# Transforming u for both halves of a column block in one step of the feed

## The chip, the cores and the metric

The kernel runs on one core of a Trainium2 chip. TensorE (PE in the profile) multiplies matrices, its weight loads are counted apart (PEld); VectorE (DVE), ScalarE (ACT) and GpSimd (POOL) work on tiles; SyncE (SP) issues nearly all transfers. The metric is the device time of one execution in microseconds, of which the median of several runs is taken.

## What is computed

Two mixers read the same input `u` (2048 rows of 448) and a gate per row mixes them. The first is a state-space convolution: a kernel `K` of 2048 taps per channel is built from 256 decaying complex modes and convolved with `u` by FFT. The second is attention in four segments of 512 rows with a memory that is carried from segment to segment.

```python
# A: state-space convolution
P = exp((A * dt)[:, :, None] * pos)            # 448 x 256 x 2048
K = 2 * einsum("dn,dnl->dl", C, P).real
a = irfft(rfft(u, 2L) * rfft(K, 2L))[:L] + u * D_skip
# B: four segments, 16 heads of 28
q, k, v = x @ wq, x @ wk, x @ wv
for s in range(4):
    a_dot = softmax(q_s k_s^T * scale + causal) v_s
    a_mem = (phi(q_s) M) / (phi(q_s) z)
    o_s = g * a_mem + (1 - g) * a_dot
    M, z = M + phi(k_s)^T v_s, z + sum(phi(k_s))
b = o @ wo
out = sigmoid(u . gate_w) * a + (1 - that) * b
```

## The kernel before

**Two halves.** The first half (to about 444 us of the profile) builds the taps of `K`, makes all projections q, k, v, the memory of each segment, and the first step of the transform of `u`. The second half loads what the first left in HBM, transforms `K` (`transform_k`, matmuls `ps_a<-kb,s1k`), finishes the FFT and runs the attention. Its first rows are the loads of the mask `mk` (L1573) and of `qu` and `ku` (L1393), all issued by SP.

**The taps.** `first_half` (L309) runs 56 steps n. A step has `turns` (eight small bf16 matmuls into `ps_arg`), `trig` on ACT (two rounds and one sine, tile `cs`), `product` on DVE (X at L393, Y at L397, L398, L399) and `sums` on PE (64 matmuls `ps_k<-Y,X`). Behind every fourth step stands a group: ACT loads its exponential table, makes six `decay` tiles (EY, EX) from `ps_arg`, the taps are copied to `kb` (L420), and ACT loads the table for sines again. ACT and DVE run in the order in which the code calls them (`k.strict`); PE always does.

**The feed.** All other work of the first half comes out of a generator, `project` (L680), a step at a time. `Feed.spend` (L483) releases steps until their modelled cost has used up the allowance `RATES` of the stage; a step yields its cost, and "pe" means a hold: two units of a projection are in PSUM, and no more is released until `exps` makes room. For each segment s the generator loads four tiles `xin` (L852), turns them on PE into `xh` and `xl` (L1382), makes `values`, then units of q and k (nine matmuls `ps_m<-xh,w` and `ps_m<-xl,w`). A unit's result is emptied by `e` and `hi` on ACT and by `ph` and `lo` on DVE (L765, L767); `memory` adds four matmuls `ps_m<-v,pkT`, emptied on DVE into `tm` and `macc` (L810, L811).

**The transform of u.** `transform_u` (L513) is a second generator, the `filling`. A step of it takes one half h of one column block w: one fp32 matmul on the 64 rows of that half, `ps_m<-ut,s1u`, into a buffer of the PSUM tag "m", a copy to `gs` (on ACT, or on DVE while `k.exps` is set) and a DMA to GU in HBM (L538). There are 32 steps. They are taken at the start of each segment but the first, in twos on either side of `memory` in the units called light (L907 on), by `spend` where a hold leaves allowance over, by `fill` at the end of the steps (L450, L456), and what is left by `rest`. The blocks `ut` are loaded two ahead, in three buffers. `gs` takes three buffers of its own, and from w = 12 on the half h = 1 takes one of the four `xin` buffers.

**PSUM.** The tag "m" has three buffers in the first half (L1507). Transposes, values, units, memory and the transform of u all take them in turn; a matmul waits until the buffer that it is given has been emptied.

Of the kernel before, what the change touches and what calls it, by code (L numbers as in the profile page):

```python
# [308 lines left out]
def first_half(nc, k, gy, feed):  # L309
# [21 lines left out]
    def load(J):  # L331
        if J < NJ:
            load_decay(J)
            load_phase(J)
# [26 lines left out]
    def turns(n):  # L361

        J, c = divmod(n, 2)
        arg[n] = pt = k.ps("arg")
        for nt in range(2):
            r, kw = rows(nt)
            k.mm(pt[:, nt], lt[J][r, c], k.ct[r, 0], start=True, stop=False, **kw)
        for i in range(2):
            for nt in range(2):
                r, kw = rows(nt)  # L370
                k.mm(pt[:, nt], k.one[r], k.mag[r, i : i + 1].broadcast_to([64, 512]), start=False, stop=False, **kw)
        for nt in range(2):
            r, kw = rows(nt)
            k.mm(pt[:, nt], lt[J][r, c], k.ct[r, 1], start=False, stop=True, **kw)

    def trig(n):

        pt = arg.pop(n)
        cs[n] = t = gw.tile([128, 2, 2, 2, 256], F32, tag="cs", name="cs", bufs=2)
        pv = pt.rearrange("p t (w c) -> p t w c", w=2)  # L380
        act(t[:, 1].rearrange("p w t c -> p t w c"), pv, AF.Sin, scale=TWO_PI)
        act(t[:, 0].rearrange("p w t c -> p t w c"), pv, AF.Abs)
        fl = t[:, 0].rearrange("p w t c -> p (w t c)")
        act(fl, fl, AF.Sin, bias=k.bhp, scale=-TWO_PI)

    def product(n):
        J, c = divmod(n, 2)
        t = cs.pop(n)
        X = gw.tile([128, 2, 2, 256], F32, tag="X", name="X", bufs=2)
        Y = gw.tile([128, 2, 16, 64], F32, tag="Y", name="Y", bufs=2)  # L390
        XY[n] = X, Y
        ex = EX[J][:, :, 256 * c : 256 * c + 256].unsqueeze(1).broadcast_to([128, 2, 2, 256])
        v.tensor_tensor(X, ex, t[:, :, 0], ALU.mult)  # L393
        ey = EY.pop((J, c)).rearrange("p t (d c) -> p (t d) c", c=64)
        y = t[:, :, 1].rearrange("p r t (d c) -> p r (t d) c", c=32)
        lo = ey[:, :, :32].unsqueeze(1).broadcast_to([128, 2, 16, 32])
        v.tensor_tensor(Y[:, :, :, :32], lo, y[:, :, :, ::-1], ALU.mult)  # L397
        v.tensor_tensor(Y[:, 0, :, 32:], ey[:, :, 32:], y[:, 0], ALU.mult)  # L398
        v.scalar_tensor_tensor(Y[:, 1, :, 32:], ey[:, :, 32:], -1.0, y[:, 1], ALU.mult, ALU.mult)  # L399
# [39 lines left out]
    for n in range(2 * NJ):  # L439
        if n < 4:  # L440
            load(n + 2)
        elif n % 2 == 0:
            load(n // 2 + 4)
        if n % 4 < 3:
            turns(n + 1)
        trig(n)
        feed.spend(1.7 * RATES[n // 4])
        product(n)
        if n == 2 * NJ - 1:
            feed.fill(2)  # L450
        if n % 4 > 0:
            sums(n - 1)
        if n % 4 == 3 and n + 1 < 2 * NJ:
            decays(n // 4 + 1)
            turns(n + 1)
    feed.fill(4)  # L456
    sums(2 * NJ - 1)


# [53 lines left out]
def transform_u(nc, k, up, pp):  # L513

    uv = k.u.rearrange("(n h w) d -> h n w d", h=2, w=16)
    guv = k.GU.rearrange("k r (h w) d -> h (k r) w d", h=2)
    def load(w):
        ut = up.tile([128, D], F32, tag="ut", name="ut", bufs=3)
        for h in range(2):
            nc.sync.dma_start(ut[64 * h : 64 * h + 64], uv[h, :, w])  # L520
        return ut

    uts = {0: load(0), 1: load(1)}
    for w in range(16):
        if w < 14:
            uts[w + 2] = load(w + 2)
        ut = uts.pop(w)
        for h in range(2):
            pt = k.ps("m")
            k.mm(  # L530
                pt[:, :D], k.s1u[64 * h : 64 * h + 64], ut[64 * h : 64 * h + 64],
                start=True, stop=True,
            )

            where, tag, bufs = (pp, "xin", 4) if w >= 12 and h else (up, "gs", 3)
            gs = where.tile([128, D], F32, tag=tag, name="gs", bufs=bufs)
            k.copy(gs, pt[:, :D], AF.Copy)
            nc.sync.dma_start(guv[h, :, w], gs)  # L538
            yield 0.9


def transform_k(nc, k, fp):
# [137 lines left out]
def project(nc, k, pp, early, filling):  # L680
# [72 lines left out]
    def high(u, pt):  # L753
        hi = pp.tile([128, SEG], F32R, tag="hi", name="hi", bufs=2)
        if u[2] == 0:
            copy(hi, pt, AF.Copy)
        else:
            copy(hi, pt, AF.Identity, bias=k.po)
        return hi
# [78 lines left out]
    def remember():  # L838
        while pending:
            u, ph = pending.pop(0)  # L840
            yield from memory(u, ph)
            yield 1.0 - 0.4 * u[2]

    for s in range(NSEG):
        if s > 0:
            yield -next(filling, 0.1)
        xh = pp.tile([112, 4, SEG], F32R, tag="xh", name="xh")
        xl = pp.tile([112, 4, SEG], F32R, tag="xl", name="xl")
        for t in range(4):
            xin = pp.tile([128, D], F32, tag="xin", name="xin", bufs=4)  # L850
            with k.issue_after(holds[s]) if s in holds else ExitStack():
                nc.sync.dma_start(xin, k.u[SEG * s + 128 * t : SEG * s + 128 * t + 128])  # L852
            pt = k.ps("m")
            for kt in range(4):
                k.tr(
                    pt[:112, 128 * kt : 128 * kt + 128], xin[:, 112 * kt : 112 * kt + 112], k.ident
                )
            pv = pt[:112].rearrange("p (k q) -> p k q", k=4)
            ts_ = slice(128 * t, 128 * t + 128)
            copy(xh[:, :, ts_], pv, AF.Copy)  # L860
            v.tensor_tensor(xl[:, :, ts_], pv, xh[:, :, ts_], ALU.subtract)
            yield -1.0 if s == 0 or t % 2 else 1.0
        yield from remember()
        if s > 0:
            yield from values(s, xh, xl, range(1))
        if s == 0:
            split = weights()
            for _ in range(4):
                yield next(split)

        if s == 0:
            plain = [(s, h, 0) for h in range(4)]
            units = [(s, h, 1) for h in range(4)]
        elif s == 3:
            plain = [(s, h, 1) for h in range(4)]
            units = [(s, h, 0) for h in range(4)]
        else:
            plain = []
            units = [(s, h, m) for h in range(4) for m in range(2)]
        order = plain + units if s == 0 else units + plain  # L880
        after = dict(zip(order, order[1:] + [None]))
        x = (xh, xl)

        def rest_of(us):
            for u in us:
                pt = yield from matmuls(u, x)
                load_w(after[u])
                store(u, pt, high(u, pt))
                yield -0.7

        if s == 0:
            yield from values(s, xh, xl, range(4))
            for x_ in split:
                yield -0.3
                k.turn_over(k.ps("m"), 3)
                yield 0.6
            yield from rest_of(plain)
        for i in range(0, len(units), 2):
            us = units[i : i + 2]
            pts = []  # L900
            light = i == 2 if s == 0 else i > 2 and s < 3
            if s > 0 and i == 2:
                yield from values(s, xh, xl, range(1, 4))
                store_v(s)
            for u in us:
                if pts:
                    for _ in range(2 if light else 0):  # L907
                        yield -next(filling, 0.1)
                    yield from remember()
                    for _ in range(2 if light else 0):  # L910
                        yield -next(filling, 0.1)
                pts.append((yield from matmuls(u, x)))
                load_w(after[u])
                yield 0.65
            yield "pe"
            es, his, phs = [], [], []
            for u, pt in zip(us, pts):
                es.append(raised(pt))
                his.append(high(u, pt))
            for u, pt, e, hi in zip(us, pts, es, his):  # L920
                phs.append(phi(pt, e))
                store(u, pt, hi)
            if s == 0 and i == 0:
                store_v(s)
            pending += zip(us, phs)
            yield 0.1
        if s == 3:
            yield from rest_of(plain)
# [692 lines left out]
```

## Time and profile before

| | |
|---|---|
| median of 3 runs | 852.42 us (850.0 to 855.2) |
| span of the profiled execution | 850.4 us |
| PE busy | 750.1 us, 88% of the span |
| DVE busy | 582.0 us, 68% |
| ACT busy | 538.6 us, 63% |
| POOL busy | 171.8 us, 20% |
| DMA moved | 152.98 MB, 180 GB/s in the mean |

The shares are means over two halves with different limits. A stage is read from the table of windows (busy time of each engine between two times, with PEclk, the clock that the throttle granted to TensorE, 1.00 being full speed), and in it from the timeline: start, duration, engine, line, tiles and, in brackets, the idle time before a row and what ended it. The chain of waits follows the work that ended last back from the end of the kernel. Several instructions in a row of one kind are one line of the timeline (x64).

### The profile page before, as it was taken

What the parts mean: (1) busy time and instruction counts of PE and PEld (TensorE: products, weight loads), DVE (VectorE), ACT (ScalarE), POOL (GpSimd) and SP (SyncE); (2) the same over time, 40 slices, a digit from 0 to 9 for tenths busy, and PEclk for the clock granted to TensorE, in tenths of its full rate; (3) what the DMA queues carried; (4) which work ended last, traced back from release to release, by engine and by line L of the source; (5) the groups of instructions that cost most, each with busy time, mean ns of one, the idle gap of its engine ahead of it and who ended that gap; (6) DMA issues with size and microseconds to landing.
All of it is one profiled execution on the core that took longest, in us unless ns stands there. A gap on an engine that the chain in (4) does not pass through costs nothing.

```text
span 850.4 us, 19021 instructions
## 1 busy us (share of the span) xinstructions
PE 750.1 (88%) x7608; PEld 405.1 (48%) x7608; DVE 582.0 (68%) x1143; ACT 538.6 (63%) x638; POOL 171.8 (20%) x217
## 2 busy tenths in 40 slices
PE   1686987998879989899988999989997998988997
PEld 1363655764546655566643444434443444343443
DVE  8878678767788676876687765656565757563474
ACT  4867889799998989898863255554453444521320
POOL 5314111011110111001110121341115113331110
PEclk9589999999999989799999899999999999979899
DMA  9347853325642346314558967667466645654872
GB/s 248 91 108 237 247 186 112 99 91 172 197 143 85 104 153 200 132 46 149 178 202 349 349 221 235 204 220 233 118 219 220 194 152 182 210 205 152 223 231 97
DMA packets 88290, 152.98 MB, mean 180 GB/s; under 512 B 20626, under 2 KB 57162, under 8 KB 88154
## 3 DMA queue, kind: packets, MB, share of 16 engines
q1 hardware_dynamic: 79130, 140.83, 51.7%
q10 hardware_dynamic: 7424, 9.18, 3.1%
q0 software_dynamic: 1648, 1.76, 0.8%
q8 instruction: 60, 0.98, 0.5%
q14 instruction: 28, 0.23, 0.1%
HBM read 90.87 MB, written 60.63 MB: 178 GB/s over the span
## 4 chain that ended last, share of the span: by engine, by line
PE 54%; ACT 16%; DVE 15%; DMA 7%; issue 6%; POOL 1%; SPq 1%; ACTq 0%; DVEq 0%; POOLq 0%
PE ps_a L1379 19%; PE ps_m L1379 17%; PE ps_pv L1379 8%; ACT cs L1344 7%; PE ps_arg L1379 5%; PE ps_k L1379 3%; DVE jk L994 3%; DVE Y L397 2%; ACT L1344 2%; PE ps_m L1382 2%; DVE Y L398 1%; DVE X L393 1%; DMA xt<-in_A_u 1%; ACT EX L1344 1%; DMA ident<-in_c_id 1%
## 5 line engine op out<-in xcount | busy, mean ns | idle before, releaser
L994 DVE CUSTOM_DVE_ANT_0 jk<-ps_a,mk 128x512 f32<-128x512 f32 (+3 forms) x256 | 124.9, 488 | 71.0 <-PE ps_a L1379 63.7
L1024 ACT ACTIVATE PT<-ps_a 128x1024 f32<-128x1024 f32 (+1 forms) x96 | 84.5, 881 | 118.6 <-PE ps_a L1379 112.0
L359 POOL TENSOR_TENSOR EX<-EX,cab 128x1024 f32<-128x1024 f32 x28 | 53.5, 1913 | 309.1 <-ACT EX L1344 244.8
L1344 ACT ACTIVATE cs<-ps_arg 128x1024 f32<-128x1024 f32 x111 | 107.3, 1021 | 0.6 <-DVE Y L398 0.3
L1379 PE MATMUL ps_m<-xh,w 112*128 112x512 f32 x256 | 92.9, 412 | 0.4 <-DVE lo L765 0.4
L1379 PE MATMUL ps_a<-qu,ku 32*128 32x512 f32 (+3 forms) x768 | 89.3, 353 | 1.7 <-DVE mx L994 1.4
L1035 POOL TENSOR_SCALAR_AFFINE_SELECT PT<-PT 128x256 f32<-128x256 f32 (+1 forms) x96 | 46.5, 485 | 206.5 <-ACT PT L1024 206.4
L393 DVE TENSOR_TENSOR X<-EX,cs 128x1024 f32<-128x1024 f32 x56 | 68.3, 1220 | 25.4 <-ACT cs L1344 25.4
L1379 PE MATMUL ps_k<-Y,X 128*32 128x64 f32 x3584 | 64.1, 226 | 9.0 <-DVE Y L398 8.8
L1379 PEld LDWEIGHTS ps_k<-Y,X 128*32 128x32 f32 x3584 | 54.9, 113 | 35.2 <-DVE Y L398 16.1
L397 DVE TENSOR_TENSOR Y<-EY,cs 128x1024 f32<-128x1024 f32 x56 | 70.0, 1250 | 0.0
L1379 PEld LDWEIGHTS ps_a<-qu,ku 32*128 32x128 f32 x768 | 62.4, 194 | 12.4 <-DVE mx L994 4.7
L1344 ACT ACTIVATE cs<-cs,bhp 128x1024 f32<-128x1024 f32 x56 | 64.5, 1151 | 1.8
L399 DVE SCALAR_TENSOR_TENSOR Y<-EY,cs 128x512 f32<-128x512 f32 x56 | 41.0, 732 | 31.2 <-ACT cs L1344 29.1
L1344 ACT ACTIVATE EY<-ps_arg 128x1024 f32<-128x1024 f32 x52 | 53.1, 1031 | 11.1 <-PE ps_arg L1379 10.1
L1379 PEld LDWEIGHTS ps_m<-xh,w 112*128 112x128 f32 x256 | 48.0, 188 | 19.7 <-issue 7.6
L1379 PE MATMUL ps_a<-ku,qu 32*128 32x512 f32 (+3 forms) x256 | 46.0, 394 | 12.3 <-DVE mx L994 9.9
L1379 PE MATMUL ps_arg<-ct,lh 64*128 64x512 bf16 x224 | 43.6, 387 | 9.0 <-ACT cs L1344 5.7
L1379 PE MATMUL ps_m<-xl,w 112*128 112x512 f32 x128 | 50.3, 393 | 0.0
L1379 PEld LDWEIGHTS ps_a<-ku,qu 32*128 32x128 f32 x256 | 22.2, 189 | 58.7 <-DVE mx L994 27.0
L1379 PEld LDWEIGHTS <-lh 64*128 64x128 bf16 x392 | 22.2, 95 | 53.4 <-issue 39.8
L606 DVE TENSOR_TENSOR pr<-ps_a,ks 128x896 f32<-128x896 f32 x32 | 34.8, 1087 | 17.7 <-PE ps_a L1379 17.0
(212 smaller groups left out, 1395.3 us busy)
## 6 DMA issues: line engine op xcount, KB each, us to landing
w<-WD SPq DMA_DIRECT2D x32, 448.0 KB, 4.7
qu<-QD SPq DMA_DIRECT2D x16, 512.0 KB
ku<-KD SPq DMA_DIRECT2D x16, 512.0 KB
GU<-gs SPq DMA_DIRECT2D x32, 224.0 KB, 2.5
GK<-gs SPq DMA_DIRECT2D x8, 896.0 KB, 5.1
gk<-GK SPq DMA_DIRECT2D x32, 224.0 KB, 4.7
gu<-GU SPq DMA_DIRECT2D x32, 224.0 KB, 3.7
BB<-bs ACTq DMA_DIRECT2D x16, 448.0 KB, 2.6
```

The costliest lines, as they stand in the source:

```text
L359: nc.gpsimd.tensor_tensor(o, o, cab, ALU.mult)
L393: v.tensor_tensor(X, ex, t[:, :, 0], ALU.mult)
L397: v.tensor_tensor(Y[:, :, :, :32], lo, y[:, :, :, ::-1], ALU.mult)
L398: v.tensor_tensor(Y[:, 0, :, 32:], ey[:, :, 32:], y[:, 0], ALU.mult)
L399: v.scalar_tensor_tensor(Y[:, 1, :, 32:], ey[:, :, 32:], -1.0, y[:, 1], ALU.mult, ALU.mult)
L606: nc.vector.tensor_tensor(pr[c], pt, ks.pop(c), ALU.mult)
L994: v.tensor_tensor_reduce(junk[:, :n], pt[:, x, o : o + n], k.mk[:, SEG - n :], 1.0, -3e38, ALU.add, ALU.max, mx[:, 3 - t, h : h + 1],)
L1024: nc.scalar.activation(PT[:, 2 * hp : 2 * hp + 2, 512 * b : 512 * b + n], pt[:, :, :n], AF.Exp, scale=SCALE)
L1035: nc.gpsimd.affine_select(sl, sl, pat, ALU.is_ge, 0.0, base=0, channel_multiplier=-1)
L1344: x = op(*args, **kw)
L1379: tc.keep_in_program_order(nc.tensor.matmul(*args, **kw))
L1382: tc.keep_in_program_order(nc.tensor.transpose(*args))
```

## The change

A step of the transform of u now makes both halves of a column block: two PSUM buffers are taken, the two matmuls are issued one behind the other on the upper and the lower 64 rows of TensorE, then the two copies and the two DMAs. There are 16 steps, and a step's modelled cost is 1.5 where two steps of before had 1.8. Where the code took two steps it takes one, where four two; at the start of a segment and in `spend` it takes one step as before, which is now two halves.

```diff
         if n == 2 * NJ - 1:
-            feed.fill(2)
+            feed.fill(1)
...
-    feed.fill(4)
+    feed.fill(2)
     sums(2 * NJ - 1)
...
-        for h in range(2):
-            pt = k.ps("m")
+        pts = [k.ps("m") for _ in range(2)]
+        for h, pt in enumerate(pts):
             k.mm(
                 pt[:, :D], k.s1u[64 * h : 64 * h + 64], ut[64 * h : 64 * h + 64],
                 start=True, stop=True,
             )
-
+        for h, pt in enumerate(pts):
             where, tag, bufs = (pp, "xin", 4) if w >= 12 and h else (up, "gs", 3)
             gs = where.tile([128, D], F32, tag=tag, name="gs", bufs=bufs)
             k.copy(gs, pt[:, :D], AF.Copy)
             nc.sync.dma_start(guv[h, :, w], gs)
-            yield 0.9
+        yield 1.5
...
                 if pts:
-                    for _ in range(2 if light else 0):
+                    for _ in range(1 if light else 0):
                         yield -next(filling, 0.1)
                     yield from remember()
-                    for _ in range(2 if light else 0):
+                    for _ in range(1 if light else 0):
                         yield -next(filling, 0.1)
```

The instructions stand elsewhere in the queues than before, at three places above all. The first is the memory update of segment 1, ACT's queue: `cs` are the tiles of `trig`, `gs` the copies of the transformed u, `pkT` belongs to `memory`. Before:

```order
L1344 ACTIVATE pkT<-ps_m 128x512
L1344 ACTIVATE cs<-ps_arg 128x2x2x256 x2
L1344 ACTIVATE cs<-cs,bhp 128x1024
L1344 ACTIVATE gs<-ps_m 128x448
L1344 ACTIVATE cs<-ps_arg 128x2x2x256 x2
L1344 ACTIVATE cs<-cs,bhp 128x1024
L1344 ACTIVATE gs<-ps_m 128x448
L1344 ACTIVATE cs<-ps_arg 128x2x2x256 x2
```

With the change:

```order
L1344 ACTIVATE pkT<-ps_m 128x512
L1344 ACTIVATE cs<-ps_arg 128x2x2x256 x2
L1344 ACTIVATE cs<-cs,bhp 128x1024
L1344 ACTIVATE gs<-ps_m 128x448 x2
L1344 ACTIVATE cs<-ps_arg 128x2x2x256 x2
L1344 ACTIVATE cs<-cs,bhp 128x1024
```

The two copies, which stood behind two steps of `trig`, now stand behind one, and the next `trig` is queued behind both.

The second is the start of segment 3, SP's queue: `xin` are the four tiles that the segment's transposes read, QD and KD the stores of q and k. Before:

```order
L770 DMA QD<-hi 128x512
L852 DMA xin<-in_A_u 128x448 x2
L770 DMA KD<-hi 128x512
L852 DMA xin<-in_A_u 128x448 x2
L770 DMA QD<-lo 128x512
```

With the change:

```order
L770 DMA QD<-hi 128x512
L770 DMA KD<-hi 128x512
L770 DMA QD<-lo 128x512
L538 DMA GU<-gs 128x448
L770 DMA KD<-lo 128x512
L852 DMA xin<-in_A_u 128x448
L538 DMA GU<-gs 128x448
L852 DMA xin<-in_A_u 128x448 x2
L322 DMA lh_92<-SD 48x128 x2
L852 DMA xin<-in_A_u 128x448
```

The four loads, which stood among the stores of an earlier pair of units, now stand behind the stores of the last pair of u.

The third is the end of the first half, PE's queue, with the sums of the last three steps and the first matmuls of the second half. Before:

```order
L1379 MATMUL ps_m<-ph,macc_205 128x512
L1379 MATMUL ps_m<-ph,macc_206 128x512
L1379 MATMUL ps_m<-ut,s1u 128x448
L1379 MATMUL ps_k<-Y,X 32x64 x32
L1379 MATMUL ps_m<-ut,s1u 128x448 x3
L1379 MATMUL ps_k<-Y,X 32x64 x32
L1379 MATMUL ps_m<-ut,s1u 128x448 x4
L1379 MATMUL ps_k<-Y,X 32x64 x32
L1379 MATMUL ps_m<-ut,s1u 128x448
L1379 MATMUL ps_a<-kb,s1k 128x448 x16
```

With the change:

```order
L1379 MATMUL ps_m<-xl,w 128x512
L1379 MATMUL ps_m<-xh,w 128x512
L1379 MATMUL ps_k<-Y,X 32x64 x32
L1379 MATMUL ps_m<-ph,macc_205 128x512
L1379 MATMUL ps_m<-ph,macc_206 128x512
L1379 MATMUL ps_k<-Y,X 32x64 x64
L1379 MATMUL ps_a<-kb,s1k 128x448 x16
```

The nine halves of u that stood between the last sums are gone from there (all 16 pairs come before the transposes of segment 3), and the nine matmuls of one unit, the last two of which are shown, have come in ahead of them.

## The prediction

> **What bounds the kernel now.** I read the page first, then the windows of the first half, where the whole change lies, then the timeline at the places where u is transformed, and last the chain of waits at the end of that half.
>
> ```profile
> span 850.4 us, 19021 instructions
> PE 750.1 (88%) x7608; PEld 405.1 (48%) x7608; DVE 582.0 (68%) x1143; ACT 538.6 (63%) x638; POOL 171.8 (20%) x217
> 100.00:240.00 140.00, 125.37 (x1888) 80.72 (x1888) 108.70 (x152) 127.75 (x146) 19.12 (x10) 1.00 0.45 145
> 240.00:252.00 12.00, 9.76 (x165) 5.60 (x166) 11.08 (x18) 10.82 (x15) 1.99 (x2) 0.86 0.52 170
> 252.00:352.00 100.00, 92.87 (x1274) 59.05 (x1270) 72.25 (x101) 88.77 (x100) 13.32 (x7) 0.93 0.40 129
> 352.00:364.00 12.00, 9.83 (x165) 5.49 (x166) 10.94 (x17) 10.67 (x15) 2.03 (x2) 0.86 0.44 150
> ```
>
> The columns of the windows are length, busy time of PE, PEld, DVE, ACT and POOL, granted clock, DMA share and GB/s. The page's 88% of PE would make TensorE the bound and any saving on it a gain. The windows say otherwise for the first half: from 100 to 240 us ACT is busy 127.75 of 140.00 (91%), PE 125.37 (90%), DVE 78%; from 252 to 352 PE has 93%, ACT 89%. PE and ACT are level, and work passes from one to the other. In the two 12 us windows, the exponential phases at the start of segments 2 and 3, DVE and ACT are at about 90% and PE at 82%, and the clock fell to 0.86.
>
> **What the pairing can save.** These are all matmuls of u, the copies, and places where one, two and three halves run behind one another (a half is fp32 and has two passes, hence x2 and x64):
>
> ```profile
> L1379 PE MATMUL ps_m<-ut,s1u 64*128 64x448 f32 x64 | 31.4, 598 | 3.1 <-DVE lo L767 1.5 <-DMA ut<-in_A_u 0.7 <-DVE lo L765 0.5
> L1344 ACT ACTIVATE gs<-ps_m 128x448 f32<-128x448 f32 x19 | 10.2, 542 | 7.2 <-PE ps_m L1379 7.2
> L1344 DVE COPY gs<-ps_m 128x448 f32<-128x448 f32 x13 | 8.0, 619 | 2.7 <-PE ps_m L1379 2.2 <-DMA KD<-hi 0.5
> 432.23 1.02 PE L1379 MATMUL ps_m<-ut,s1u 64*128 64x448 f32 x2 [0.73 <-DVE lo L767]
> 434.20 1.77 PE L1379 MATMUL ps_m<-ut,s1u 64*128 64x448 f32 x6
> 543.57 1.02 PE L1379 MATMUL ps_a<-gk,cf 64*128 64x448 f32 x4 [0.36 <-DVE pr L606]
> ```
>
> One half alone takes 1.02 us from start to end. Three take 1.77: one of them added 0.75, another nothing. At 543.57 four passes of the same shape on both row halves take the same 1.02 as two. So a pair whose buffers are both free costs what one half costs, and saves 0.75 us of PE: 16 x 0.75 = 12.0 us at most. The copies are the same 32, of 0.54 us on ACT or 0.62 on DVE.
>
> But both buffers must be free at once, and the tag "m" has three. By the order of the allocations, which the code fixes, at none of the 16 pairs does the second half find a buffer that was surely empty before. For seven it is one that DVE empties with `lo` of a unit just made; for five it is the one that `tm` or `macc` of the memory update empties; for four it is the one of their own first half, so that the second half waits for the first one's copy. PE works in order and stands still meanwhile, with sums or decays queued behind.
>
> The Trainium skill, "TensorEngine Tiling (Array Packing)", section "Restrictions and Gotchas", names this as the price of row tiling: row tiles write to different PSUM banks, so the pressure on PSUM grows. That weighs against the change; the numbers that follow are from rows alone.
>
> **Seven pairs behind `lo`.** The wait of 0.73 us at 432.23 is such a wait of a single half, so a pair may lose 0.73 or gain 0.75: for seven -5.3 to +5.1. The holds make PE wait for `lo` in any case, so I take near nothing: +0.8.
>
> **Five pairs in the memory updates.** Segment 1, before:
>
> ```profile
> 204.62 1.16 PE L1379 MATMUL ps_m<-v,pkT 128*128 128x128 f32 x8 [1.11 <-ACT pkT L1344]
> 205.71 1.02 PE L1379 MATMUL ps_m<-ut,s1u 64*128 64x448 f32 x2
> 207.18 0.28 DVE L810 TENSOR_TENSOR tm<-ps_m,bm 128x128 f32<-128x128 f32 x1
> 207.48 0.53 ACT L1344 ACTIVATE gs<-ps_m 128x448 f32<-128x448 f32 x1
> 207.90 1.93 ACT L1344 ACTIVATE cs<-ps_arg 128x1024 f32<-128x1024 f32 x2
> 210.92 0.52 ACT L1344 ACTIVATE gs<-ps_m 128x448 f32<-128x448 f32 x1
> 211.18 1.22 DVE L393 TENSOR_TENSOR X<-EX,cs 128x1024 f32<-128x1024 f32 x1
> 211.34 1.93 ACT L1344 ACTIVATE cs<-ps_arg 128x1024 f32<-128x1024 f32 x2
> ```
>
> One half stood behind `v,pkT`, and its copy filled a slot of ACT. Now the second half follows at once, but its buffer comes free when `tm` ends: 207.18 + 0.28 = 207.46. Its 0.9 to 1.0 us end it at 208.4, its copy lasts to 208.9, and `trig`, queued behind both copies, starts at 208.9 instead of 207.90: +1.0. The later copy at 210.92 is gone (-0.45). X at 211.18, which waits for `trig`, and everything behind it moves by 0.5 to 1.0. Meanwhile `sums` and `turns` wait behind the second half on PE. Five times 0.7: +3.5 (0 to 5.2).
>
> **The starts of the segments.** A start takes one step, now a pair instead of a half, and further ones by `spend`. Where the second half waits for its own first one's copy, a matmul and a copy come on top: 1.02 + 0.53 = 1.55. For segment 1 I take this: +1.55 (0 to 1.55). Segment 2 gets four copies where it had one, 3 x 0.54 = 1.6 us on an ACT that has 1.2 us left in its 12 us window: +1.0 (0.4 to 2.6). Segment 3 has more:
>
> ```profile
> 327.61 0.90 SPq L852 DMA_DIRECT2D xin<-in_A_u  x2
> 351.80 1.28 ACT L1344 ACT_TABLE_LOAD   x1
> 356.01 0.58 ACT L1344 ACTIVATE gs<-ps_m 128x448 f32<-128x448 f32 x1
> 356.65 1.09 PE L1382 MATMUL ps_m<-ident,xin 128*112 128x128 f32 x8 [2.17 <-ACT gs L1344]
> 359.89 1.02 ACT L1344 ACTIVATE EY<-ps_arg 128x1024 f32<-128x1024 f32 x1 [0.46 <-PE ps_arg L1379]
> 361.38 1.03 ACT L1344 ACTIVATE EY<-ps_arg 128x1024 f32<-128x1024 f32 x1 [0.47 <-PE ps_arg L1379]
> 363.82 1.28 ACT L1344 ACT_TABLE_LOAD   x1
> ut<-in_A_u SPq DMA_DIRECT2D x32, 112.0 KB, 3.6
> ```
>
> Before, `xin` was loaded 29 us ahead (327.61) and turned at 356.65, 4.85 us after the table load. Now the loads stand in SP's queue behind the stores of the last pairs, and their buffers are those of the halves h = 1. In the same clock: the first copy of the pair at 356.0, the second half 1.02 later and its copy to 358.1, a decay of 1.05, two copies of the last pair to 360.2, a store of `lo` and the issue to 360.9, and 3.6 us to landing (of the loads of u, `ut`): 364.5, 12.6 after the table load instead of 4.85. Three of the six decays stand behind these transposes on PE; with 0.55 for the first transposes, the step of 359.89 to 361.38 twice and one decay, the phase ends 16.8 after the table load instead of 363.82 - 351.80 = 12.0: +4.8 (0 if the loads are not late, 7.6 if all that they are late remains).
>
> **Sum of the loops.** The steps between have fewer halves, and one unit leaves for the end of the half: nine matmuls, some 2 us of PE where PE has up to 93%, -1.5. So 0.8 + 3.5 + 1.55 + 1.0 + 4.8 - 1.5 = 10.15. ACT at 90% hides little of it, but PE and DVE catch up some: I let three quarters through, +7.6. In the 12 us windows a gap of 2.17 us went with a clock of 0.86, so a longer gap may cost (1 - 0.86) x 12 = 1.7 us again: +1.5 (0 to 2).
>
> **The end of the first half** gains:
>
> ```profile
> 436.71 3.85 DMA ut<-in_A_u
> 441.69 1.03 PE ps_k L1379 x64
> 442.72 0.96 PE ps_m L1379 x2
> 443.71 0.55 ACT gs L1344
> 444.69 0.38 SPq L1573
> 445.62 5.47 DMA ku<-KD
> 451.18 0.85 PE ps_a L1379 x5
> 439.15 0.68 DVE L398 TENSOR_TENSOR Y<-EY,cs 128x512 f32<-128x512 f32 x1
> ```
>
> This is the chain of waits but for its last row, which is of the timeline. The last halves wait for `ut` (3.85 us), the last sums for them, the load of `mk` (L1573) for the last half's copy and store, and the attention's first rows at 451.18 for `ku` behind it. With no half left, the last sums wait for the last product only, 439.15 + 0.68 = 439.83, end at about 440.9, and `mk` goes out at 441.1 instead of 444.69: -3.6 (0 if the unit that has come in delays the products as much).
>
> Total: +7.6 + 1.5 - 3.6 = +5.5 on 850.4, 855.9. The profiled execution is 2.0 under the median of the runs, so 852.42 + 5.5 = **858 us**.
>
> **Rivals.**
> 1. *The pairs run together as meant.* For it: 434.20 shows that the array does it, and 12 of the 16 pairs hold a second buffer of another kind. Against it: what empties that buffer comes late. Saved would be 12.0 us of PE, of which half lies on the path while PE and ACT are level, 6, and 3.6 at the end, less some 2 at segment 3: 850.4 - 7.6 and 2.0 more is 845. The Trainium skill, "TensorE: Matmul & The Clock Gate", "Part 3: Packing small matmuls", says that matmuls start and end strictly in order. Held to for every pass, a pair would take three passes and save half of the 0.75; the row of 543.57 does not agree with that.
> 2. *Absorbed.* The waits of PE fall where it would wait for ACT in any case, and the loops lose 3.6, what the end gains: 852.
> 3. *Segment 3 decides* (slower, more than forecast). One mechanism: the loads of `xin` land at 12.6 us after the table load, and the whole 7.6 us of lateness stays, since ACT with its exponentials, DVE with its products and the unit behind the transposes all start that much later; it decides as soon as the landing is more than 4 us behind 356.65. The loops' 10.15 become 10.15 + 2.8 = 12.95, nothing of it is caught up, the clock costs 2, and the end gives 3.6: +11.4, 864.
>
> **How the numbers follow.** The forecast (the waits outweigh, 855 to 861) has 0.50, rival 1 0.15, rival 2 0.20, rival 3 0.15. A measurement tells about 0.5% from no change, 4.3 us. Faster: rival 1 and a little of rival 2, 0.17. Same: the rest of rival 2 and the forecast's lower edge, 0.22. Slower: 0.61. The range reaches from above rival 1 to beyond rival 3: 848 to 867; the forecast's own is 854 to 862.
>
> **What would show it.** In the windows of the changed kernel: PE's idle time before `ps_m<-ut,s1u` well over 3.1 us, released by `tm`, `lo` and `gs`; rows of u that read x4 in 1.02 us would speak for rival 1. At a memory update, two copies in a row with the wait between them and `trig` about 1.0 later. At segment 3, the loads of `xin` issued some 9 us after the table load, the transposes waiting for a DMA, and about 17 us from one table load to the next. At the end, `mk` issued right behind the last sums. Wrong it would be if the transposes of segment 3 wait for nothing, or if ACT's idle time in the loops does not grow.

## The result, and the profile after

The change makes the kernel slower by 4.0%: 885.62 us in the median of four runs (880.94 to 890.62) against 851.62 for the kernel before (four runs) on the same chip, a ratio of 1.0399 with a 95% interval of 1.0335 to 1.0463. The forecast was 858 us. The profiled execution has a span of 880.3 us, 29.9 more than before.

The head of the page, and the groups of the transform of u (its matmuls, and the first DVE step that empties a held unit):

```profile
span 880.3 us, 19020 instructions
PE 760.1 (86%) x7608; PEld 408.7 (46%) x7608; DVE 585.7 (67%) x1139; ACT 539.0 (61%) x642; POOL 171.6 (19%) x217
L1379 PE MATMUL ps_m<-ut,s1u 64*128 64x448 f32 x64 | 31.1, 626 | 18.4 <-DVE tm L810 8.2 <-ACT gs L1344 5.9 <-DVE lo L765 2.1
L779 DVE TENSOR_SCALAR e<-e 128x512 f32<-128x512 f32 x24 | 10.0, 421 | 25.6 <-ACT e L1344 25.6
```

No engine has more to do worth naming (PE 10 us, DVE 4, ACT 0.4). PE's idle time ahead of the matmuls of u has grown from 3.1 to 18.4 us, and it is ended by `tm` on DVE, `gs` on ACT and `lo` on DVE: the three kinds of PSUM buffer that the prediction had named. DVE waits 25.6 us for `e` of held units, before 7.2.

Where the time goes is read best between the table loads of ACT. Both kernels have 32 of them, at the same places in the program; the difference of their starts in the two traces says how far the one is behind. The last stands at the end of the first half:

```profile
440.58 1.28 ACT L1344 ACT_TABLE_LOAD   x1
```

```profile
469.54 1.28 ACT L1344 ACT_TABLE_LOAD   x1
```

The change is 28.96 us behind there, so all of its loss but 0.9 us lies in the first half. The table shows how much each stretch between two table loads lengthened, as the difference of its two lengths, and the clock granted to TensorE in it, before and with the change; the stretches left out change by 2.9 at most, either way, and by 3.4 together.

| stretch of before, us | what it holds | change | clock before | clock with the change |
|---|---|---|---|---|
| 132.4 to 143.3 | exponentials, start of segment 1 | +3.8 | 1.00 | 0.77 |
| 199.2 to 214.5 | four steps, memory update | +4.0 | 1.00 | 0.91 |
| 224.5 to 239.8 | four steps, memory update | +4.1 | 1.00 | 0.91 |
| 239.8 to 251.9 | exponentials, start of segment 2 | +5.8 | 0.86 | 0.71 |
| 334.7 to 351.8 | four steps, memory update | +3.0 | 0.80 | 0.83 |
| 351.8 to 363.8 | exponentials, start of segment 3 | +8.3 | 0.86 | 0.75 |
| up to 419.7 in all | | +32.4 | | |
| 419.7 to 440.6 | the last steps, no u any more | -3.4 | 1.00 | 1.00 |

In five of the six places where time is lost, TensorE also got less clock than before. In the sixth, 334.7 to 351.8, the trace of before was itself at 0.80, so what is lost there is more than the 3.0 shown.

**A memory update** of segment 1, the timeline of PE, ACT and DVE in the change:

```profile
214.03 1.16 PE L1379 MATMUL ps_m<-v,pkT 128*128 128x128 f32 x8
215.12 1.02 PE L1379 MATMUL ps_m<-ut,s1u 64*128 64x448 f32 x2
219.21 1.02 PE L1379 MATMUL ps_m<-ut,s1u 64*128 64x448 f32 x2 [3.08 <-DVE tm L810]
220.16 1.70 PE L1379 MATMUL ps_k<-Y,X 128*32 128x64 f32 x64
216.17 0.54 ACT L1344 ACTIVATE gs<-ps_m 128x448 f32<-128x448 f32 x1 [0.28 <-PE ps_m L1379]
220.26 0.54 ACT L1344 ACTIVATE gs<-ps_m 128x448 f32<-128x448 f32 x1 [3.55 <-PE ps_m L1379]
220.70 1.94 ACT L1344 ACTIVATE cs<-ps_arg 128x1024 f32<-128x1024 f32 x2
215.99 1.22 DVE L393 TENSOR_TENSOR X<-EX,cs 128x1024 f32<-128x1024 f32 x1
218.87 0.28 DVE L810 TENSOR_TENSOR tm<-ps_m,bm 128x128 f32<-128x128 f32 x1
221.98 0.69 DVE L399 SCALAR_TENSOR_TENSOR Y<-EY,cs 128x512 f32<-128x512 f32 x1 [2.50 <-PE ps_k L1379]
```

Its matmuls end at 215.2, but DVE makes `tm` at 218.87, behind a whole product that begins at 215.99. Until then the second half has no buffer: PE stands 3.08 us, ACT 3.55 with `trig` (`cs`) behind the second copy, and DVE itself 2.50 later, for sums that PE held back behind that half. Three engines wait in a ring for one small step on DVE.

**The start of segment 3** in the change, ACT, DVE, PE and SP:

```profile
375.86 1.28 ACT L1344 ACT_TABLE_LOAD   x1
381.02 0.54 ACT L1344 ACTIVATE gs<-ps_m 128x448 f32<-128x448 f32 x1 [1.11 <-PE ps_m L1379]
381.46 0.59 ACT L1344 ACTIVATE e<-ps_m 128x512 f32<-128x512 f32 x1
390.86 1.02 ACT L1344 ACTIVATE EY<-ps_arg 128x1024 f32<-128x1024 f32 x1 [3.81 <-PE ps_arg L1379]
396.18 1.28 ACT L1344 ACT_TABLE_LOAD   x1
382.08 0.43 DVE L779 TENSOR_SCALAR e<-e 128x512 f32<-128x512 f32 x1 [3.24 <-ACT e L1344]
389.21 1.07 PE L1382 MATMUL ps_m<-ident,xin 128*112 128x128 f32 x4 [3.28 <-DMA xin<-in_A_u]
386.08 0.44 SPq L852 DMA_DIRECT2D xin<-in_A_u  x1
```

The loads of `xin` go out 10.2 us after the table load and the transposes begin 13.35 after it (12.6 were forecast). What was not forecast stands ahead of them: `e` of a held unit comes behind two copies of u on ACT, and DVE waits 3.24 us for it. The phase takes 20.3 us instead of 12.0.

**The end of the first half**, SP and PE in the change:

```profile
473.43 0.33 SPq L1573 DMA_DIRECT2D mk<-in_c_mk  x1
480.68 0.74 PE L1379 MATMUL ps_a<-ku,qu 32*128 32x512 f32 x2
```

From the last table load to the attention's first matmul it is 11.1 us, before 10.6 (451.18 - 440.58); the 3.4 us are won in the stretch ahead of that load.

And four of the 16 pairs do run together, all of them among the seven that the prediction had put behind `lo`, as this one, four passes in 0.92 us (x4, PE):

```profile
203.17 0.92 PE L1379 MATMUL ps_m<-ut,s1u 64*128 64x448 f32 x4
```

### The profile page after: what moved, and what is told of

The parts are those of the page before. It is cut to its first block, busy times and chain, and to the rows that moved or that the text cites. A ratio compares the mean times of both kernels' runs of the same rounds, so it can differ in the third digit from the quotient of the medians.

```text
span 880.3 us, 19020 instructions
## 1 busy us (share of the span) xinstructions
PE 760.1 (86%) x7608; PEld 408.7 (46%) x7608; DVE 585.7 (67%) x1139; ACT 539.0 (61%) x642; POOL 171.6 (19%) x217
## 4 chain that ended last, share of the span: by engine, by line
PE 60%; DVE 15%; ACT 13%; DMA 5%; issue 4%; SPq 1%; POOL 0%; DVEq 0%; ACTq 0%
PE ps_m L1379 21%; PE ps_a L1379 20%; PE ps_pv L1379 8%; ACT cs L1344 5%; PE ps_arg L1379 5%; PE ps_k L1379 5%; DVE jk L994 3%; DVE Y L397 3%; DVE X L393 2%; PE ps_m L1382 2%; DVE Y L398 1%; ACT L1344 1%; DMA dn<-pvs 1%; DMA winv<-in_B_wv 1%; ACT EX L1344 1%
## 5 line engine op out<-in xcount | busy, mean ns | idle before, releaser
L1379 PE MATMUL ps_m<-xh,w 112*128 112x512 f32 x256 | 95.5, 420 | 0.3 <-DMA w<-WD 0.3
L1379 PE MATMUL ps_k<-Y,X 128*32 128x64 f32 x3584 | 66.7, 231 | 23.3 <-DVE Y L398 23.2
L1379 PEld LDWEIGHTS ps_k<-Y,X 128*32 128x32 f32 x3584 | 57.1, 116 | 45.1 <-DVE Y L398 27.8
L397 DVE TENSOR_TENSOR Y<-EY,cs 128x1024 f32<-128x1024 f32 x56 | 70.0, 1250 | 0.0
L1379 PE MATMUL ps_arg<-ct,lh 64*128 64x512 bf16 x224 | 41.6, 386 | 8.2 <-ACT cs L1344 6.9
L1379 PEld LDWEIGHTS ps_a<-ku,qu 32*128 32x128 f32 x256 | 22.3, 190 | 56.7 <-DVE mx L994 25.6
```

Of the source, the lines that this page charges most:

```text
L1379: tc.keep_in_program_order(nc.tensor.matmul(*args, **kw))
```

## The experiments

Two theories stood at the start. M: the second half waits for `tm`, and DVE has `tm` behind a product. S: the starts of the segments cost most. Against both stood P: two halves at once hold two of three buffers and cost time wherever they stand. Ratios, each with its 95% interval, are to the kernel before on the same chip; the times in us come from several chips. "Behind" is how far the last table load lies behind that of before (28.96 us in the change). It is read from one execution of each kernel, and the fourth run below shows how far two executions of the same order can differ in it: 6 us.

**Pairs in the light units alone.** From the kernel before:

```diff
-                    for _ in range(2 if light else 0):
-                        yield -next(filling, 0.1)
+                    if light:
+                        yield -two()
```

`two` takes two halves and yields 1.5, at both places of the light units.

> Two halves of u are made in one step only in the light units (around the memory updates); at the segment starts, in spend and in the last fills a step is one half, as before. Theory M (the second half waits for tm, and DVE has tm behind a whole product): here the order leaves tm ahead of the product X, so the memory updates cost little; within 5 us of before, 847 to 857. Theory S (the segment starts cost most, 18 of the 32 us): also near before, since the starts are as before. Theory P (two halves at once hold two of three PSUM buffers and cost it wherever they stand): 12 to 15 us over before, 864 to 868.

Measured: 1.0242 (1.0164 to 1.0321), 878.47 us, 24.7 us behind. M and S both fall as stated: neither the late `tm` nor the pairs at the starts are in this kernel, yet it loses 2.4%. P had forecast a loss, but a time of 864 to 868 us, and 878 were measured: none of the three accounts for it. PE waits 10.7 us ahead of u. The trace shows a second order that has turned over. At the start of segment 2 DVE, before, made the product X first and emptied the held units behind it, without a wait:

```profile
240.00 1.21 DVE L393 TENSOR_TENSOR X<-EX,cs 128x1024 f32<-128x1024 f32 x1
242.88 0.75 DVE L779 TENSOR_SCALAR e<-e 128x512 f32<-128x512 f32 x2
```

These are DVE, PE and ACT at that place with pairs in the light units:

```profile
255.01 0.43 DVE L779 TENSOR_SCALAR e<-e 128x512 f32<-128x512 f32 x1 [1.89 <-ACT e L1350]
257.88 0.74 DVE L767 SCALAR_TENSOR_TENSOR lo<-ps_m,po,hi 128x512 fp32r<-128x512 f32 x1
258.54 1.22 DVE L393 TENSOR_TENSOR X<-EX,cs 128x1024 f32<-128x1024 f32 x1
261.41 2.40 DVE L399 SCALAR_TENSOR_TENSOR Y<-EY,cs 128x512 f32<-128x512 f32 x1
264.46 1.10 PE L1388 MATMUL ps_m<-ident,xin 128*112 128x128 f32 x4 [3.92 <-DVE xl L867]
266.14 1.02 ACT L1350 ACTIVATE EY<-ps_arg 128x1024 f32<-128x1024 f32 x1 [4.36 <-PE ps_arg L1385]
```

DVE first waits for `e` of a held unit, empties both units to 258.6, and only then makes the group's last product; what comes after that (the emptying of the transposes, the sums) is late, and ACT's exponentials wait 4.36 us.

**Pairs at the starts and in spend alone.** From the kernel before:

```diff
         if s > 0:
-            yield -next(filling, 0.1)
+            yield -two()
...
             self.due -= next(self.filling, 0.0)
+            self.due -= next(self.filling, 0.0)
```

> Two halves in one step only at the segment starts and in spend; in the light units and the last fills one half, as before. Theory S: the starts cost 14 to 18 us, of which the end of the half gives some back: 862 to 868, with the phase between the two table loads of segment 3 some 16 to 20 us. Theory M: only what the starts cost beside tm, also over before, but the change's other half of the loss is missing: 860 to 866, and no wait of a matmul of u for tm over 1.5 us. If both were wrong and only the pairing in the light units cost time: 850 to 855.

Measured: 1.014 (1.0061 to 1.0218), 866.48 us, 11.6 behind. This is what S had forecast: 866 lies in its 862 to 868, and the phase of segment 3 takes 16.8 us, in its 16 to 20. The starts cost time by themselves: those of segments 1 and 3 lengthen by 4.0 and 4.8 us, with 4.3 more in the stretch behind the latter, that of segment 2 not at all. S is thus right in what the starts cost; that they cost most is not shown, since the pairs in the light units alone lost more.

**The change with `tm` ahead of the product.**

```diff
+        with k.issue_after(k.tm) if hasattr(k, "tm") else ExitStack():
+            v.tensor_tensor(X, ex, t[:, :, 0], ALU.mult)
...
-            v.tensor_tensor(tm, pm[:, :128], k.bm, ALU.mult)
+            k.tm = v.tensor_tensor(tm, pm[:, :128], k.bm, ALU.mult).ins
```

The other products of a step and segment 0's `macc` are tied in the same way.

> The change with one order added: DVE makes tm ahead of the product X that follows it in the code, as in the kernel before; matmuls, copies and their order on PE are the same. Theory M: the four waits for tm of 1.5 to 3.6 us fall to 1 or less, and the time falls by 8 to 12 us against the change, to 873 to 878. Theory S or P: the waits move to the next buffer or the time stays, 882 to 889.

Measured: 1.0177 (1.0102 to 1.0251), 871.88 us, 16.6 behind. PE and DVE at the same memory update as above:

```profile
215.18 1.02 PE L1381 MATMUL ps_m<-ut,s1u 64*128 64x448 f32 x2
216.37 1.02 PE L1381 MATMUL ps_m<-ut,s1u 64*128 64x448 f32 x2 [0.17 <-DVE tm L812]
216.03 0.28 DVE L812 TENSOR_TENSOR tm<-ps_m,bm 128x128 f32<-128x128 f32 x1
```

`tm` comes at 216.03 and the wait is 0.17 instead of 3.08 us. The three stretches with a memory update lengthen by 1.1, 1.6 and -0.2 instead of 4.0, 4.1 and 3.0, and the last table load is 12.4 us earlier than the change's. By the two ratios the gain is larger, 2.2% or 19 us, and their intervals do not meet; M had forecast 8 to 12 us. So the place of `tm` in DVE's queue accounts for some two fifths of the loss by the traces and for over half of it by the ratios; its size is known no better than that.

**Each half's copy behind its own matmul**, the rest as the change:

```diff
-        pts = [k.ps("m") for _ in range(2)]
-        for h, pt in enumerate(pts):
+        for h in range(2):
+            pt = k.ps("m")
...
-        for h, pt in enumerate(pts):
             where, tag, bufs = (pp, "xin", 4) if w >= 12 and h else (up, "gs", 3)
```

> The change with each half's copy written behind its own matmul instead of both matmuls first; steps, places and number of halves in a step are the change's. If issuing the two matmuls one behind the other matters by itself (they run together on the two row halves, or hold two buffers at once), the time differs by 3 us or more from the change's. If only where and how many halves are made in a step matters, as theories M and S have it: 880 to 890, the same as the change.

Measured: 1.0389 (1.0316 to 1.0461), 890.13 us, 35.0 behind. The ratio is that of the change, but the run decides less than was hoped: in the two traces the instructions of the first half stand in the same order on PE, ACT, DVE and SP. Only the writing was changed, not the queues, so whether the two matmuls cost time by standing together on PE is not tested by it. It serves as a second execution of the change: 35.0 us behind instead of 29.0, of which 4.0 had come up before 132 us. Differences of a few us between two values of "behind" are therefore no more than hints.

**The copies of the last blocks in buffers of their own**, added to the kernel with `tm` first:

```diff
-            where, tag, bufs = (pp, "xin", 4) if w >= 12 and h else (up, "gs", 3)
+            where, tag, bufs = up, "gs", 3
```

> e3_tm_first, and the copies of the last four blocks go to the three gs buffers instead of the xin buffers, so that the loads of xin for segment 3 stand early in SP's queue again. If the late loads cost what the transposes waited for them (3.3 and 0.5 us in the change), the phase between the two table loads of segment 3 falls from 19.9 to about 16 and the time by 3 to 5 us against e3_tm_first, to 867 to 869. If the pairs' own waits set that phase, it stays at 19 to 20 us and the time at 870 to 874.

Measured: 1.0185 (1.0132 to 1.0237), 867.52 us, 13.3 behind. SP's loads and the phase between the two table loads of segment 3:

```profile
340.73 0.90 SPq L854 DMA_DIRECT2D xin<-in_A_u  x2
```

```profile
364.82 1.28 ACT L1346 ACT_TABLE_LOAD   x1
380.57 1.28 ACT L1346 ACT_TABLE_LOAD   x1
```

The loads stand 24 us ahead of that phase again, and it takes 15.75 us instead of 19.9, as expected if the late loads cost time. They cost 4.2 us there with what the clock adds (0.67 in the phase with late loads, 0.78 without), of the change's 8.3. In the ratio this doesn't show: 1.0185 against 1.0177.

**No pairs at the starts**: the change with `tm` first, a group's last product ahead of the emptying of held units, and these lines out:

```diff
-        if s > 0:
-            yield -next(filling, 0.1)
...
-        if self.due > 1.5 and (self.held or self.done) and self.waiting:
-            self.due -= next(self.filling, 0.0)
```

> The change with pairs only in the light units and after the last step: none at the segment starts and none in spend, so twelve halves come at the end; tm ahead of the product that follows it (as e3_tm_first), and a group's last product ahead of the emptying of the held units. If the starts cost most of what e3_tm_first still loses: the phases at the three starts return to 11 to 12 us, the loops lose 2 to 5 us in all, the end grows by 2 to 4, and the time is 856 to 862. If the pairs in the light units cost it: 868 or more.

Measured: 1.0208 (1.0139 to 1.0278), 871.09 us, 8.4 behind. The time misses the 856 to 862 that were expected if the starts cost most, and lies where the pairs in the light units were expected to. The loops don't quite behave as expected either: they lose 6.7 us and not 2 to 5, and the three phases take 13.3, 14.6 and 14.6 us and not 11 to 12. Still it is 10 us less than the 16.7 that the kernel with buffers of its own has at 419.7 us. That is the pairs at the starts and in `spend` together with the order of the product, which the two kernels don't share either; the run below shows that this order alone can be worth more than 10 us. So what the starts cost by themselves is not separated here. The total loses in the second half: from the attention's first matmul on this kernel takes 409.1 us in its profile, before 399.2, the change 399.6. In that stretch TensorE was granted 0.91 of its clock, in the other two 0.94, and 0.91 is the lowest of all thirteen traces. Twelve halves at the end of the first half don't explain that; why the clock was lower is open.

**A group's last product ahead of the held units**, added to the kernel with pairs in the light units alone:

```diff
-        v.tensor_tensor(Y[:, 0, :, 32:], ey[:, :, 32:], y[:, 0], ALU.mult)
+        k.made = v.tensor_tensor(Y[:, 0, :, 32:], ey[:, :, 32:], y[:, 0], ALU.mult).ins
...
-        v.tensor_scalar(e, e, 1.0, None, ALU.min)
+        with k.issue_after(k.made) if hasattr(k, "made") else ExitStack():
+            v.tensor_scalar(e, e, 1.0, None, ALU.min)
```

> e1_light (pairs only in the light units, single halves elsewhere as before) with one order added: DVE makes a group's last product ahead of the emptying (min, ph, lo) of the two held units. The trace of e1_light has that product behind them in the exponential phases, and its last exponentials 4 to 5 us late behind the sums that wait for it. If this order costs e1_light its time: the phases of 13.5 to 16.3 us return to 10 to 12.5, and the time falls by 12 to 18 us, to 858 to 866. If it is that two halves hold two of three PSUM buffers, the time stays at 874 to 880.

Measured: 1.0126 (1.0069 to 1.0183), 863.36 us, 10.9 behind instead of 24.7. DVE's wait for `e`, 14.7 us in that kernel, is gone, and with it more than half of what it was behind. The time lies in the 858 to 866 that were expected if the order costs it; the intervals of the two ratios just overlap. The wait of PE ahead of u stays, half of it for `tm`:

```profile
L1386 PE MATMUL ps_m<-ut,s1u 64*128 64x448 f32 x64 | 30.8, 595 | 10.5 <-DVE tm L811 5.1 <-DVE lo L767 1.7 <-DVE lo L765 1.7
```

**The start's pair behind the transposes**: the kernel with own buffers and the product first, and `if s > 0: yield -next(filling, 0.1)` moved from the head of a segment to behind its transposes and `remember`.

> f1_own_gs with the pair at a segment's start moved behind the four transposes (and memory) of that segment, where the held units have been emptied, and a group's last product ahead of the emptying of the held units. If the starts cost time because two held units leave the pair one PSUM buffer and ACT has the unit's e and hi between the two halves, the three phases at the starts come back to 11 to 13 us and the time falls by 5 to 9 us against f1_own_gs, to 859 to 863. If the pairs cost the same wherever they stand, it stays at 865 to 870.

Measured: 1.0085 (1.0046 to 1.0124), 864.12 us, 9.1 us behind instead of 13.3, in a trace of one of its longer executions (867.67). The phases at the starts of segments 2 and 3 take 14.3 and 14.2 us, not 11 to 13. The ratio is better than the 1.0185 (1.0132 to 1.0237) of the kernel with own buffers, but two things were changed at once: the place of the pair and the order of the product. How much is the pair's is not shown.

**The last blocks of u loaded early**: the kernel before, blocks 14 and 15 loaded into `xin` buffers behind the transposes of segment 3.

```diff
-        ut = up.tile([128, D], F32, tag="ut", name="ut", bufs=3)
+        where, tag, bufs = (pp, "xin", 4) if w >= 14 else (up, "ut", 3)
+        ut = where.tile([128, D], F32, tag=tag, name="ut", bufs=bufs)
```

> The kernel before, no pairs; the last two blocks of u are loaded into xin buffers behind the transposes of segment 3, instead of into ut buffers that come free only at the end. If the gain of 3.4 us that the change has at the end of the first half comes from the halves that waited there for ut, this kernel gets most of it without the losses: from the last table load to the first matmul of the attention 7 to 8.5 us instead of 10.6, and 849 to 852 where before has 852 to 855. If the gain comes from the halves being gone, wait or not, the time is that of before.

Measured: 0.9993 (0.9957 to 1.0029): the same. From its last table load to the first matmul of the attention it is 11.2 us; that matmul now waits for `ps_a<-kb,s1k` ahead of it on PE instead of for `ku`. The run doesn't settle where the 3.4 us come from, since it puts a new wait in the place of the old one. The two blocks take two of the four `xin` buffers, which the copies of the last halves need, and the last copy on ACT ahead of the table load waits for a store:

```profile
436.87 0.54 ACT L1348 ACTIVATE gs<-ps_m 128x448 f32<-128x448 f32 x1 [1.96 <-DMA GU<-gs]
```

So it shows only that loading the blocks early in this way gains nothing.

**Pairs only ahead of the memory updates**: the kernel with the product first, the second place of the light units back to two single halves.

```diff
-                    if light:
-                        yield -two()
+                    for _ in range(2 if light else 0):
+                        yield -next(filling, 0.1)
```

> f3_product_first with the five pairs behind the memory updates taken as two single halves again, as before; the five pairs ahead of them stay. If what f3_product_first still loses (11 us at the last table load) is the second half's wait for tm and macc, that loss falls to 1 to 4 us and the time is 853 to 857, within 0.5% of before. If pairs cost time wherever they stand, half of the loss stays: 858 to 862. If pairs with free buffers gain what they save on PE (0.75 us each): 848 to 851.

Measured: 0.9988 (0.9936 to 1.0039), 1.2 us ahead of before at the last table load and 2.3 behind the control that follows. The ratio's interval doesn't meet the one of the kernel with the product first (1.0069 to 1.0183), and one thing alone differs between the two. So the five pairs behind the memory updates, which wait for `tm` and `macc`, cost nearly all that was left. P falls with it: five pairs in the light units still stand, and cost nothing that can be measured. PE's wait ahead of u is that of before again:

```profile
L1386 PE MATMUL ps_m<-ut,s1u 64*128 64x448 f32 x64 | 30.8, 607 | 2.8 <-DVE lo L767 1.7 <-DMA ut<-in_A_u 0.5 <-ACT gs L1351 0.3
```

**Control**: the kernel before with the product tied as above, and no pairs.

> The kernel before with the one order of f3_product_first added (a group's last product ahead of the emptying of the held units) and no pairs. It tells what that order costs or gains by itself: if the comparisons above are fair, nothing, 851 to 856 like before; if the order is a gain of its own, 850 or less.

Measured: 0.9994 (0.9959 to 1.003). The order costs and gains nothing by itself. At its last table load it is 3.4 us ahead of the profile of before, and that is the clock's doing: the stretches of before from 307.7 and from 334.7 took 17.08 and 17.09 us at a granted clock of 0.80, and in the control 15.30 and 15.29 at 1.00, while another stretch of the control, from 224.5 on, took 17.07 at 0.80 where before had 15.30. No version is measurably faster than the kernel before.

## Why the prediction was wrong

The direction held, the size did not: +5.5 us forecast, +29.9 in the profile and +34.0 in the medians.

*Which buffers.* Right, to the count. None of the 16 pairs was sure of a second buffer: of the seven behind `lo` four ran together and three waited, five waited for `tm` or `macc`, and four for the copy of their own first half.

*Five pairs in the memory updates, +3.5.* This is the step that failed. It took the time of `tm` from the timeline of before (207.18, right behind the end of a product) and moved only the second half to it, so that this would start 1.75 us behind the first (205.71 to 207.46). It started 4.09 behind (215.12 to 219.21). But the change moves `tm` too. The description of the kernel says that ACT and DVE run in the order in which the code calls them; for the products and for `tm` on DVE that is wrong, since `first_half` and `project` call `nc.vector` and leave their order to the scheduler. DVE's queue, before:

```
L399 SCALAR_TENSOR_TENSOR Y<-EY,cs 128x16x32
L810 TENSOR_TENSOR tm<-ps_m,bm 128x128
L811 TENSOR_TENSOR macc_204<-macc_204,tm 128x128
L393 TENSOR_TENSOR X<-EX,cs 128x1024
L397 TENSOR_TENSOR Y<-EY,cs 128x32x32
L398 TENSOR_TENSOR Y<-EY,cs 128x16x32
```

and with the change:

```
L393 TENSOR_TENSOR X<-EX,cs 128x1024
L397 TENSOR_TENSOR Y<-EY,cs 128x32x32
L398 TENSOR_TENSOR Y<-EY,cs 128x16x32
L810 TENSOR_TENSOR tm<-ps_m,bm 128x128
L811 TENSOR_TENSOR macc_204<-macc_204,tm 128x128
```

At three of the five memory updates with a pair, those of the stretches of 4.0, 4.1 and 3.0 us, `tm` went behind X, L397 and L398, 2.9 us by the rows (215.99 to 218.87). In the kernel before nobody waited for `tm` soon; with the pair the second half, and behind it sums, `trig` and the next product, do. The five second halves wait 9.4 us on PE (1.28, 3.08, 3.08, 0.50 and 1.50). The prediction looked at the queues of PE, ACT and SP only. Undoing the order gives back 12.4 us in the trace and 2.2% in the ratio.

*The starts, +7.35.* Right in kind, too small: 3.8, 5.8 and 8.3, 17.9 in all, lower clock included. For segment 3 the late loads were forecast at 4.8 and cost 4.2. (By the prediction's own rows the terms there add up to 17.2 us and not 16.8, so +5.2, and the lateness to 7.75 and not 7.6; the forecast would move by a few tenths.) Missing was that the first half's copy stands on ACT behind `e`, `hi` and a decay of the held units (or these behind the copies): at segment 1 PE waited 2.66 us for it, where the prediction had one copy, 0.53.

*Three quarters let through.* Wrong. The lag at the table loads grows at each of these places and is not made up later: the loops end 32.4 us behind.

*The clock, +1.5.* Of the right kind, and likely too small: sums behind such a wait took 1.70 us (220.16) where those of before took 1.10. From 132 us to the last table load, length times the clock that was lacking comes to about 10 us before and 21 with the change. A stretch that lacked 3.4 us by this count (17.09 at 0.80) was 1.8 longer than at 1.00; by that measure, an estimate, some 5 us of the loss are the clock's. No run separates it: these us lie within the terms above, since the low clock of the rows looked at stands behind their waits.

*The end, -3.6.* Right in size: -3.4, but in the stretch up to the last table load, and not behind it, where `mk` was to go out sooner (from that load to `mk` it is 3.9 us, before 4.1). The agreement of the size is luck as far as the path goes. Whether the wait for `ut` made it is open.

*Rival 1* (all pairs together, 845) and *rival 2* (absorbed, 852) fall for the change; with pairs only where the second buffer comes free in time, rival 2 is what happens, 0.9988. *Rival 3*, segment 3 alone, had the right side and one of six places. Of the Trainium skill's two rules, the pressure of row tiling on PSUM ("TensorEngine Tiling (Array Packing)", "Restrictions and Gotchas") is borne out, with 15.3 us more of idle time ahead of these matmuls.

As far as the traces go, the 32.4 us divide so: 12.4 by the order of `tm`, 3.3 by the loads of `xin`, 10 by the pairs at the starts and in `spend` together with the order of the product, and 6.7 left. For what is left the best evidence is the run with pairs only ahead of the updates, in which the second half's wait for `tm` and `macc`, and nearly all of the loss, is gone. The four numbers are differences of single traces, and the two traces of one order differed by 6 us, so only the first and the third are clear of that.

## What to carry to other kernels

Pair work on the halves of the array only where the second PSUM buffer is free by then: 0.75 us of PE was to be won by a pair, and 3.08 us were lost at each of two places where it had to wait, since all that stood behind it on PE waited too. When a change moves instructions, read the queue of the engine that frees the buffer, not only those that the edit names. Where a scheduler places work, a step that nobody waited for may be late without harm until something is put behind it; then tie its place. And before two traces are compared by a few us, look at the granted clock of the stretch, and at how far two executions of one order differ.

## What was not expected of the hardware

In the kernel with pairs in the light units three steps of a product on DVE behind 100 us took 2.40 us instead of 0.68, one of them at 261.41 above; the kernel before has none there. GpSimd ran a tensor operation at that time, which itself took longer than the 1.91 us that it has elsewhere:

```profile
260.95 2.31 POOL L359 TENSOR_TENSOR EX<-EX,cab 128x1024 f32<-128x1024 f32 x1 [22.20 <-ACT EX L1350]
269.47 1.91 POOL L359 TENSOR_TENSOR EX<-EX,cab 128x1024 f32<-128x1024 f32 x1 [6.21 <-ACT EX L1350]
```

In all three cases DVE's step ends 0.55 us behind GpSimd's operation, as if it had stood still until then, and the order of DVE decides whether the two meet. The Trainium skill, "SBUF — State Buffer", section "Terms", says that VectorE and GpSimd share a pair of ports under an exclusive lock and the loser is blocked; the trace agrees, with 1.7 us lost on DVE beside an operation that takes 1.91 alone.

PE ran passes of u at half speed after a wait of 2.66 us, PE's timeline at the start of segment 1 in the change:

```profile
135.70 0.54 PE L1379 MATMUL ps_m<-ut,s1u 64*128 64x448 f32 x1
138.90 1.11 PE L1379 MATMUL ps_m<-ut,s1u 64*128 64x448 f32 x1 [2.66 <-ACT gs L1344]
139.81 0.95 PE L1379 MATMUL ps_m<-ut,s1u 64*128 64x448 f32 x1
```

The granted clock is 0.50 from 138.9 to 143.0. So a wait of PE can cost more than its length: the matmuls behind it take up to twice as long for a while. It isn't always so, and no length of a wait is a safe bound here: behind the wait of 3.08 us above the passes of u still took 1.02, and the sums that follow them were slow; in the kernel before the clock fell to 0.50 at 313.5 behind waits of 0.71 and 1.11 us, and in the control it stayed at 1.00 in that stretch.
